# Softcap attention with soft-MoE slots on one core: queries and keys cast by their transfers, a second exponential tile per batch on VectorE

## The chip, the core and the metric

The kernel runs on one core of a Trainium2 chip. The metric is the device time of one execution in microseconds; 317.23 us is the median of seven runs of the kernel before.

## What is computed

Eight batches of twelve heads attend over 448 positions of 64 channels. The scores are capped by a tanh, so no running maximum is needed (the cap is 30). The result, seen as 3584 tokens of 768 channels, goes through a soft mixture of experts with 32 slots: the slots' softmax runs over all tokens, so the expert layers can only start when the attention of all batches is done.

```python
scores = cap * tanh((q @ k.T) / 8 / cap)          # per batch and head
attn = exp(scores) / sum(exp(scores))
x = (attn @ v) laid out as (3584, 768)
logits = x @ phi                                  # 32 columns
d = softmax over tokens of logits; slots = d.T @ x
out_e = relu(slots_e @ w1_e) @ w2_e               # 8 experts, 4 slots each
out = softmax over slots of logits @ slot_out
```

## The kernel before, in words

**Tiling.** A quad is four heads of one batch, so a batch has three quads and the kernel 24. A quad's q, k and v lie in SBUF with 128 partitions: two heads share the two halves of the partitions, and the two pairs of a quad (h = 0, 1) lie side by side in the free dimension. A pair has seven key tiles, which makes 336 score tiles of 128 x 448; six of them are a chunk, and there are 56 chunks (NCH), seven to a batch.

**The main loop** (L523) has one step for each chunk j, and each step has slots named 0, a, b, c and d in which other work is put. The fixed part of a step is: the score matmuls of the next chunk in two halves (`qk_chunk`, L260), the tanh of this chunk in two halves on ScalarE (`tanh_chunk`, L272, from PSUM), the exponential of the chunk before in one instruction on ScalarE (`exp_chunk`, L284, in place in SBUF), and the products with v of the pair that is complete (`pv_pass`, L335), each half followed by its normalisation on VectorE (`norm`, L324). [...] Everything else is put into slots by hand with `at(step, slot, function)` (L428 to L494): for a quad its casts, its transposes and its v cast (`quad_in`, L440), the transposes and logits of x, the sums of the slots, the weights' loads (`wjobs`, slot b), and filler matmuls (`spare`, L433) on the constant tile ones.

**Buffers that order the work.** Scores have two PSUM buffers, so a half of the next chunk waits for the tanh two halves back. There is one PSUM buffer for the transposes and small products (psT, tag T) and one for the products with v and the fillers (psV, tag pv). Exponentials have four SBUF buffers.

**Queries and keys.** `load` (L162) brings a quad's q or k as float32 through SyncE's queue; `cast` (L224) makes it bfloat16 on VectorE and issues the load of the next quad; `transp` (L232) makes seven 128 x 128 transposes on TensorE and copies them from PSUM on VectorE. The first quad has its own finer path (`first_half`, L200). v comes through SyncE's queue and is cast by GpSimd (`vcast`, L244), which waits until the products with the v tile of two quads back are done.

**The exponential on VectorE.** For the chunks in `shared` (L289) VectorE does the first of the six tiles with seven instructions (`poly_exp`, L291, in three parts), and ScalarE's instruction takes five tiles instead of six. Before, these are the chunks with j mod 7 = 3 from j = 10 on: seven chunks.

**The expert weights** are cast by their transfers, which GpSimd issues. What does not fit in SBUF goes to DRAM as bfloat16 (w2d) and comes back by 20 transfers of 384 KB through SyncE's queue (w2t, L631) into the SBUF that the attention's pools leave. The pools are stacked: ld, cst, ldv, qk, vb0, exps, vb1, xs before. The tail's pool starts at the place of ld, with hpad (4096 bytes of each partition) and then the 20 w2t tiles of 3072 bytes each; a w2t transfer waits until the tiles in whose place it lies are done with.

**The tail** is layer 1, layer 2 in two column halves (`layer2`, L673), and the output: ten tiles in halves (`half_tile`, L696), then pairs of whole tiles. Layer 2's second half needs all w2t tiles; the first eight half tiles are issued between its groups.

Of the kernel before, what the change touches and what calls it, by code (L numbers as in the profile page):

```python
# [9 lines left out]
F32 = mybir.dt.float32  # L10
BF16 = mybir.dt.bfloat16
# [5 lines left out]
P = 128  # L17
HP = 64
NT = 7
DH = 64  # L20
S = 448
# [11 lines left out]
def kernel(  # L33
# [54 lines left out]
    slacc = consts.tile([P, NJ, NS], F32, name="slacc")  # L88

    w1b = [wts.tile([P, NJ, F], BF16, name=f"w1b{e}", tag="w1", bufs=E)  # L90
           for e in range(E - 1)]
    w2b = wts.tile([P, R2, D], BF16, name="w2b")


# [32 lines left out]

    att = ExitStack()
    ld = att.enter_context(tc.tile_pool(name="ld", bufs=1))
    cst = att.enter_context(tc.tile_pool(name="cst", bufs=1))  # L130
    ldv = att.enter_context(tc.tile_pool(name="ldv", bufs=1))
    qk = att.enter_context(tc.tile_pool(name="qk", bufs=2))
    vb = [att.enter_context(tc.tile_pool(name="vb0", bufs=1))]
# [22 lines left out]
                       ap=[[NT * DH, P], [2 * S * DH, 2], [1, NT * DH]])  # L156

    def raw_tile(nm):
        return (ldv if nm == "v" else ld).tile([P, 2, S], F32, name=nm + "raw",
                                               tag=nm + "raw")  # L160

    def load(nm, Q):  # L162
        if Q < NQ:
            t = raw_tile(nm)
            sp.dma_start(out=t, in_=quad_ap(nm, Q))
            raws[nm, Q] = t

    def load_first():

        for nm in "qkv":  # L170
            raws[nm, 0] = raw_tile(nm)
        kc = raws["k", 0].rearrange("p h (c d) -> p h c d", d=DH)
        kin = quad_ap("k", 0, 0).rearrange("p (c d) -> p c d", d=DH)
        sp.dma_start(out=raws["q", 0][:, 0, :], in_=quad_ap("q", 0, 0))
        for c0, c1 in ((0, CS), (CS, NT)):
            act.dma_start(out=kc[:, 0, c0:c1, :], in_=kin[:, c0:c1, :])
        for nm in "kq":
            sp.dma_start(out=raws[nm, 0][:, 1, :], in_=quad_ap(nm, 0, 1))
        t = wts.tile([P, 3, 2, S], F32, name="raw1", tag="w1", bufs=E)
        for n, nm in enumerate("kqv"):  # L180
            raws[nm, 1] = t[:, n, :, :]
            if nm == "v":
                sp.dma_start(out=raws["v", 0], in_=quad_ap("v", 0))
            sp.dma_start(out=raws[nm, 1], in_=quad_ap(nm, 1))

    def first_pieces(h, jobs):

        for stage, nm, c0, c1, eng, bank, at0 in jobs:
            copy = act.copy if eng is act else dve.tensor_copy
            cols = slice(h * HP, h * HP + HP)  # L190
            if stage == "cast":
                copy(casts[nm, 0][:, c0:c1, cols],
                     raws[nm, 0][:, h, c0 * DH:c1 * DH].rearrange("p (c d) -> p c d", d=DH))
            elif stage == "turn":
                for c in range(c0, c1):
                    pe.transpose(bank[cols, at0 + c - c0, :], casts[nm, 0][:, c, cols], ident)  # L196
            else:
                copy(qkT[nm, 0][cols, c0:c1, :], bank[cols, at0:at0 + c1 - c0, :])

    def first_half(h):  # L200
        for nm in ("k", "q"):
            if h == 0:
                casts[nm, 0] = cst.tile([P, NT, P], BF16, name=nm + "bf", tag=nm + "bf")
                qkT[nm, 0] = qk.tile([P, NT, P], BF16, name=nm + "T", tag=nm + "T")
        one = psT.tile([P, 8, P], BF16, name="ps1", tag="T")
        two = psV.tile([P, NT, P], BF16, name="ps2", tag="pv")
        if h == 0:

            first_pieces(h, (("cast", "k", 0, CS, dve, None, 0), ("cast", "q", 0, 4, dve, None, 0),
                             ("cast", "q", 4, NT, act, None, 0), ("turn", "k", 0, CS, pe, two, 0),  # L210
                             ("copy", "k", 0, CS, dve, two, 0), ("turn", "q", 0, 4, pe, one, 0),
                             ("cast", "k", CS, NT, act, None, 0),
                             ("copy", "q", 0, 4, dve, one, 0), ("turn", "q", 4, NT, pe, two, CS),
                             ("copy", "q", 4, NT, act, two, CS), ("turn", "k", CS, NT, pe, one, 4),
                             ("copy", "k", CS, NT, dve, one, 4)))
        else:
            first_pieces(h, (("cast", "k", 0, NT, dve, None, 0), ("cast", "q", 0, NT, dve, None, 0),
                             ("turn", "k", 0, NT, pe, two, 0), ("turn", "q", 0, NT, pe, one, 0),
                             ("copy", "k", 0, NT, dve, two, 0), ("copy", "q", 0, NT, dve, one, 0)))
            for nm in ("q", "k"):  # L220
                raws.pop((nm, 0)), casts.pop((nm, 0))
                load(nm, 2)

    def cast(nm, Q):  # L224
        t = cst.tile([P, NT, P], BF16, name=nm + "bf", tag=nm + "bf")
        dve.tensor_copy(t.rearrange("p c (h d) -> p h c d", h=2),  # L226
                        raws.pop((nm, Q)).rearrange("p h (c d) -> p h c d", d=DH))
        casts[nm, Q] = t
        if Q > 1:
            load(nm, Q + 1)  # L230

    def transp(nm, Q):  # L232
        src = casts.pop((nm, Q))
        home = (psV, "pv") if (nm, Q) == ("k", 1) else (psT, "T")
        ps = home[0].tile([P, NT, P], BF16, name=nm + "ps", tag=home[1])
        for c in range(NT):
            pe.transpose(ps[:, c, :], src[:, c, :], ident)  # L237
        t = qk.tile([P, NT, P], BF16, name=nm + "T", tag=nm + "T")
        dve.tensor_copy(t, ps)  # L239
        qkT[nm, Q] = t  # L240
# [45 lines left out]

    shared = [j for j in range(NCH - 2) if j % 7 == 3 and j > 7] if cap < 80 else []  # L289

    def poly_exp(j, part):  # L291
        t, bits = exs[j][:, 0, :], 2.0 ** 23
# [146 lines left out]

    def quad_in(Q, cast_k, cast_q, k_in, q_in, v_in):  # L440
        if 0 < Q < NQ:
            at(*cast_k, cast, "k", Q)
            at(*cast_q, cast, "q", Q)
            at(*k_in, transp, "k", Q)
            at(*q_in, transp, "q", Q)
            at(*v_in, vcast, Q)

    for b in range(B):
        j = b * PER
        if b == 0:  # L450
            quad_in(1, (0, "a"), (0, "b"), (0, "d"), (1, "a"), (2, "d"))
        else:
            quad_in(3 * b + 1, (j - 1, "b"), (j, "a"), (j - 1, "d"), (j, "c"), (j + 1, "d"))
        quad_in(3 * b + 2, (j + 1, "c"), (j + 2, "c"), (j + 2, "b"), (j + 2, "d"),
                (j + 4, "d"))
        quad_in(3 * b + 3, (j + 4, "a"), (j + 5, "a"), (j + 4, "d"), (j + 5, "c"),
                (j + 6, "d"))
        p = 6 * b
        at(j + 1, "d", spare, 34 if b == 0 else 10)
        at(j + 2, "d" if b == 0 else "a", spare, 4 if b == 0 else 14)  # L460
        if b:
            at(j + 2, "c", spare, 8)
        at(j + 3, "d", spare, 10)
        at(j + 4, "a", x_transp, p)
        at(j + 5, "a", x_transp, p + 1)
        at(j + 6, "a", x_transp, p + 2)
        at(j + 5, "d", logits, 3 * b)
        if b < B - 1:
            at(j + 7, "a", x_transp, p + 3)
            at(j + 8, "a", x_transp, p + 4)  # L470
            at(j + 7, "d", logits, 3 * b + 1)
            at(j + 9, "a", x_transp, p + 5)
            at(j + 9, "d", logits, 3 * b + 2)
            at(j + 11, "0", e_exp, b)
            at(j + 11, "d", slot_sums, b)
            if b < B - 2:
                at(j + 12, "d", e_transp, b)
            if b < B - 2:
                at(j + 13, "d", e_norm, b)
            if b % 2:  # L480
                at(j + 14, "d", e_sums, b // 2)
    for j in shared:
        for dj, slot, part in ((0, "a", 0), (0, "c", 1), (0, "d", 2)):
            at(j + dj, slot, poly_exp, j, part)
    for n, job in enumerate(wjobs):
        at(1 + n * (NCH - 5) // len(wjobs), "b", *job)
    for j, slot, n in ((0, "a", 10), (0, "c", 10), (1, "b", 10), (1, "c", 8)):
# [208 lines left out]
    def half_tile(n, half, home, eng):  # L696

        if n % 8 == 0:
            obs[n, half] = wts.tile([P, 8, HD], F32, name="obh", tag="w1", bufs=E)
        ob = obs[n - n % 8, half][:, n % 8, :]  # L700
        bb, c = divmod(n, NT)
        pe.matmul(home, et_tile(bb, c), so[half], start=True, stop=True)  # L702
        if eng == "dve":
            dve.tensor_scalar_mul(ob, home, winv[:, bb, c:c + 1])
        else:
            act.mul(ob, home, winv[:, bb, c:c + 1])
        store(n, half, half + 1, ob)
# [10 lines left out]
    for n0 in range(0, n2, 4):  # L718
        layer2(n0, 1)
        if n0 >= 4 and n0 % 8 == 4 and done < NH - 2:  # L720
            for eng in ("act", "dve"):
                half_tile(done, 0, bank([P, HD], name="op0"), eng)
                done += 1
    dve.tensor_copy(so[1], so_ps[1])
    for n in range(done, NH):
# [68 lines left out]
```

The softmax here doesn't subtract the row's maximum and nothing guards it: scores larger than these inputs give would overflow.

## Time and profile before

| | |
|---|---|
| median of 7 runs | 317.23 us (316.78 to 320.11) |
| the profiled execution | 317.87 us |
| its span, first to last instruction | 315.7 us |
| ScalarE busy | 281.2 us, 208 instructions |
| TensorE busy, its weight loads | 270.4 us, 191.6 us |
| VectorE, GpSimd busy | 193.6 us, 106.8 us |
| transfers | 77.68 MB written, 246 GB/s on average |

A busy engine in this profile is one that has an instruction under way. Matmuls are pipelined, so their durations overlap: what one costs the engine is the distance to the next start, not its duration. An idle time is put down to what ended it last. Times within the span are counted from its start.

### The profile page before, as it was taken

To read this page: it belongs to the slowest core of one execution; us is meant where nothing else is said; L and a number is where in the kernel's file an instruction comes from. 1 tells how busy PE (TensorE), PEld (TensorE's weight loads), DVE (VectorE), ACT (ScalarE), POOL (GpSimd) and SP (SyncE) were. 2 spreads that over 40 slices of the span, in tenths; PEclk is the share of its full clock that TensorE was granted. 3 is DMA by queue.
4 is the path that set the end of the run, shared out by engine and by line. 5 is a ranking of instruction groups with operands and counts; after the bars stand their busy time and mean duration, and the time that the engine had idled before them with its cause. 6 is when DMAs were issued, how large, how long until landed. Compare 5 with 4: busy or idle time off the path is not lost.

```text
span 315.7 us, 8844 instructions
## 1 busy us (share of the span) xinstructions
PE 270.4 (86%) x3804; PEld 191.6 (61%) x3804; DVE 193.6 (61%) x473; ACT 281.2 (89%) x208; POOL 106.8 (34%) x134
## 2 busy tenths in 40 slices
PE   8899898899889998898889989998889998998720
PEld 6667666667656665666666666666666677743400
DVE  3736565766586659565867587657766664337740
ACT  4999999999999999999999999999999999235720
POOL 2464342523543452354245415441732130200000
PEclk9999999999999999999999999999999999999995
DMA  8899999799999989999999999999999806798997
GB/s 223 261 231 234 288 256 255 159 228 264 236 210 241 265 199 236 255 215 271 191 223 276 226 253 192 244 232 261 203 227 262 221 15 213 246 397 327 391 411 304
DMA packets 57478, 77.68 MB, mean 246 GB/s; under 512 B 3808, under 2 KB 53600, under 8 KB 57440
## 3 DMA queue, kind: packets, MB, share of 16 engines
q0 software_dynamic: 30480, 25.22, 52.1%
q1 hardware_dynamic: 26672, 51.68, 48.0%
q8 instruction: 29, 0.48, 0.6%
q10 hardware_dynamic: 288, 0.23, 0.2%
q14 instruction: 9, 0.07, 0.1%
HBM read 91.32 MB, written 18.87 MB: 349 GB/s over the span
## 4 chain that ended last, share of the span: by engine, by line
ACT 60%; PE 25%; DVE 6%; issue 2%; DMA 2%; SPq 0%; DVEq 0%; ACTq 0%
ACT ex L278 30%; ACT ex L282 29%; PE pv L318 6%; PE sc L269 4%; PE junk L506 2%; PE so_ps L676 2%; PE hp L649 2%; DMA out_dram<-ob 2%; DVE xq L329 1%; PE op L702 1%; PE boot L506 1%; PE kps L237 1%; PE xps L344 1%; PE slps L407 1%; PE ps L196 1%
## 5 line engine op out<-in xcount | busy, mean ns | idle before, releaser
L278 ACT ACTIVATE ex<-sc 128x1344 bf16<-128x1344 f32 (+1 forms) x113 | 162.0, 1689 | 1.0 <-PE sc L269 1.0
L282 ACT ACTIVATE ex<-ex 128x2688 bf16<-128x2688 bf16 (+4 forms) x58 | 159.0, 2774 | 0.1
L318 PEld LDWEIGHTS <-ex 128*128 128x128 bf16 x1344 | 78.7, 97 | 21.6 <-DVE xq L329 17.9
L318 PE MATMUL pv<-vbd,ex 128*128 128x130 bf16 x1274 | 88.6, 220 | 2.7 <-ACT ex L282 0.7
L269 PE MATMUL sc<-qT,kT 64*64 64x448 bf16 x672 | 78.7, 359 | 7.8 <-ACT ex L278 7.7
L247 POOL CAST vbd<-vraw 64x896 bf16<-64x896 f32 x23 | 21.4, 929 | 104.2 <-PE pv L318 71.0
L269 PEld LDWEIGHTS <-kT 64*64 64x64 bf16 x672 | 27.2, 105 | 25.2 <-issue 7.5
L329 DVE TENSOR_TENSOR xq<-pv,rec 128x256 bf16<-128x256 f32 x91 | 38.6, 424 | 3.2
L328 DVE RECIPROCAL rec<-pv 128x4 f32<-128x4 f32 x91 | 16.5, 181 | 31.9 <-PE pv L318 31.1
L506 PEld LDWEIGHTS <-ones 128*128 128x128 bf16 x470 | 28.7, 101 | 11.6 <-DVE xq L329 8.0
L372 POOL COPY e<-E 128x512 bf16<-128x512 bf16 x9 | 7.2, 801 | 81.0 <-ACT E L366 49.0
L506 PE MATMUL junk<-ones 128*128 128x128 bf16 x433 | 31.4, 219 | 2.5 <-DVE xq L329 1.6
L239 DVE COPY kT<-kps 128x896 bf16<-128x896 bf16 x23 | 14.4, 625 | 25.3 <-PE kps L237 25.2
L109 POOL DMA_DIRECT2D w1b<-in_moe_w_dram x32 | 25.6, 803 | 0.0
L248 POOL CAST vbd<-vraw 64x896 bf16<-64x896 f32 x23 | 23.6, 1027 | 1.3
L346 DVE COPY xT<-xps 128x512 bf16<-128x512 bf16 x47 | 19.6, 417 | 3.2 <-PE xps L344 3.2
L344 PE MATMUL xps<-ident,xq 128*128 128x128 bf16 x188 | 18.1, 218 | 0.2 <-DVE zacc L383 0.2
L239 DVE COPY qT<-qps 128x896 bf16<-128x896 bf16 x23 | 14.2, 618 | 5.2 <-PE qps L237 5.2
L237 PE MATMUL kps<-ident,kbf 128*128 128x128 bf16 x161 | 12.8, 219 | 4.2 <-DVE slacc L418 2.2
L226 DVE CAST kbf<-kraw 128x896 bf16<-128x896 f32 x22 | 16.0, 728 | 0.4 <-DMA kraw<-in_k_dram 0.4
L237 PE MATMUL qps<-ident,qbf 128*128 128x128 bf16 x161 | 12.8, 219 | 3.2 <-DVE lg L360 2.7
L237 PEld LDWEIGHTS <-kbf 128*128 128x128 bf16 x161 | 10.0, 97 | 9.0 <-issue 8.3
(113 smaller groups left out, 256.9 us busy)
## 6 DMA issues: line engine op xcount, KB each, us to landing
w1b<-in_moe_w_dram POOLq DMA_DIRECT2D x32, 384.0 KB, 10.0
vraw<-in_v_dram SPq DMA_DIRECT2D x23, 448.0 KB, 6.5
qraw<-in_q_dram SPq DMA_DIRECT2D x22, 448.0 KB, 7.7
kraw<-in_k_dram SPq DMA_DIRECT2D x22, 448.0 KB, 5.7
w2d<-in_moe_w_dram POOLq DMA_DIRECT2D x20, 384.0 KB, 9.3
w2t<-w2d SPq DMA_DIRECT2D x20, 384.0 KB, 5.7
out_dram<-ob SPq DMA_DIRECT2D x8, 768.0 KB, 7.7
w2b<-in_moe_w_dram POOLq DMA_DIRECT2D x12, 384.0 KB, 9.5
```

Source lines behind the costliest of these rows:

```text
L109: pool.dma_start(out=w1b[e][:, js, fs], in_=w1r[:, e, js, fs])
L237: pe.transpose(ps[:, c, :], src[:, c, :], ident)
L239: dve.tensor_copy(t, ps)
L247: pool.tensor_copy(t[0:HP, :, :, 0:DH], raw[0:HP])
L248: pool.tensor_copy(t[HP:P, :, :, DH + 1:VW - 1], raw[HP:P])
L269: pe.matmul(sc[cs, u, 0:S], qkT["k", Q][r, c, cs], qkT["q", Q][r, :, cs], start=True, stop=True)
L278: act.activation(exs[j][:, half * CS + u0:half * CS + u1, :], sc[:, u0:u1, 0:S], ACT.Tanh, scale=qk_scale / cap)
L282: act.activation(exs[j][:, u0:u1, :], exs[j][:, u0:u1, :], ACT.Exp, scale=cap)
L318: pe.matmul(pvs[pr, half][:, n, 0:VW], exs[j][:, u, GOFF[g]:GOFF[g] + P], vbds[Q % 2][:, h, c, :], start=(c == 0 and n == 0), stop=(c == N ...
L329: dve.tensor_tensor(xq[Q][:, 2 * half:2 * half + 2, h * P:(h + 1) * P] .rearrange("p g (i d) -> p g i d", i=2), pv[:, :, :, 0:DH], rec.to_ ...
L344: pe.transpose(ps[:, g, :], xq[Q][:, g, h * P:(h + 1) * P], ident)
L506: pe.matmul(junk if home is None else home, ones, ones, start=True, stop=True)
```

## The change

- `shared` takes the chunks with j mod 7 = 1 as well as 3 (from j = 8 on), 14 chunks instead of 7. The third part of the polynomial moves from slot d of the same step to slot b (mod 1) or slot a (mod 3) of the next step.
- From quad 2 on, q and k are loaded straight into bfloat16 tiles by transfers that GpSimd issues, two buffers each; the casts on VectorE and the pool cst are gone. The loads stand in the slots where the casts stood, except those of the batch's third quad, which go from (j+1, c) and (j+2, c) to (j, d) and (j+1, c). Quads 0 and 1 are still cast by an engine; their bfloat16 tiles lie for that time in a buffer of the expert weights (so one more expert's weights gets its buffer later).
- A quad's tile now has the two pairs one after the other, so a transpose takes one pair's 128 x 64: 14 of them, with the pairs in turn, write the lower and upper half of the PSUM partitions.
- The key transposes of the third quad of a batch move from (j+4, d) to (j+3, d), and the filler there goes from 10 matmuls to 4 in the batches after the first.
- The first half tile of the output is made as two products of 192 columns in two PSUM banks, one scaled by ScalarE and one by VectorE.

```diff
     w1b = [wts.tile([P, NJ, F], BF16, name=f"w1b{e}", tag="w1", bufs=E)
-           for e in range(E - 1)]
+           for e in range(E - 2)]
...
-    cst = att.enter_context(tc.tile_pool(name="cst", bufs=1))
...
     def raw_tile(nm):
-        return (ldv if nm == "v" else ld).tile([P, 2, S], F32, name=nm + "raw",
-                                               tag=nm + "raw")
+        if nm == "v":
+            return ldv.tile([P, 2, S], F32, name="vraw", tag="vraw")
+        return ld.tile([P, 2, S], BF16, name=nm + "b", tag=nm + "raw", bufs=2)
 
     def load(nm, Q):
         if Q < NQ:
             t = raw_tile(nm)
-            sp.dma_start(out=t, in_=quad_ap(nm, Q))
+            (sp if nm == "v" else pool).dma_start(out=t, in_=quad_ap(nm, Q))
             raws[nm, Q] = t
...
     def load_first():
-        for nm in "qkv":
-            raws[nm, 0] = raw_tile(nm)
+        for nm in "qk":
+            raws[nm, 0] = [ld.tile([P, S], F32, name=f"{nm}raw{h}", tag=nm + "raw", bufs=2)
+                           for h in range(2)]
+        raws["v", 0] = raw_tile("v")
...
+        t01 = wts.tile([P, 2, 2, NT, P], BF16, name="casts", tag="w1", bufs=E)
...
-    def cast(nm, Q):
-        t = cst.tile([P, NT, P], BF16, name=nm + "bf", tag=nm + "bf")
-        dve.tensor_copy(t.rearrange("p c (h d) -> p h c d", h=2),
-                        raws.pop((nm, Q)).rearrange("p h (c d) -> p h c d", d=DH))
-        casts[nm, Q] = t
-        if Q > 1:
-            load(nm, Q + 1)
+    def cast(nm):
+        dve.tensor_copy(casts[nm, 1].rearrange("p c (h d) -> p h c d", h=2),
+                        raws.pop((nm, 1)).rearrange("p h (c d) -> p h c d", d=DH))
 
     def transp(nm, Q):
-        src = casts.pop((nm, Q))
+        src = casts.pop((nm, Q)) if Q == 1 else raws.pop((nm, Q))
...
         for c in range(NT):
-            pe.transpose(ps[:, c, :], src[:, c, :], ident)
+            if Q == 1:
+                pe.transpose(ps[:, c, :], src[:, c, :], ident)
+                continue
+            for h in range(2):
+                pe.transpose(ps[h * HP:h * HP + HP, c, :], src[:, h, c * DH:(c + 1) * DH], ident)
...
-    shared = [j for j in range(NCH - 2) if j % 7 == 3 and j > 7] if cap < 80 else []
+    shared = [j for j in range(NCH - 2) if j % 7 in (1, 3) and j > 7] if cap < 80 else []
...
     def quad_in(Q, cast_k, cast_q, k_in, q_in, v_in):
         if 0 < Q < NQ:
-            at(*cast_k, cast, "k", Q)
-            at(*cast_q, cast, "q", Q)
+            for nm, when in (("k", cast_k), ("q", cast_q)):
+                at(*when, *((cast, nm) if Q == 1 else (load, nm, Q + 1)))
...
-        quad_in(3 * b + 2, (j + 1, "c"), (j + 2, "c"), (j + 2, "b"), (j + 2, "d"),
+        quad_in(3 * b + 2, (j, "d"), (j + 1, "c"), (j + 2, "b"), (j + 2, "d"),
                 (j + 4, "d"))
-        quad_in(3 * b + 3, (j + 4, "a"), (j + 5, "a"), (j + 4, "d"), (j + 5, "c"),
+        quad_in(3 * b + 3, (j + 4, "a"), (j + 5, "a"), (j + 3, "d"), (j + 5, "c"),
                 (j + 6, "d"))
...
-        at(j + 3, "d", spare, 10)
+        at(j + 3, "d", spare, 10 if b == 0 else 4)
...
     for j in shared:
-        for dj, slot, part in ((0, "a", 0), (0, "c", 1), (0, "d", 2)):
-            at(j + dj, slot, poly_exp, j, part)
+        for slot, part in (("a", 0), ("c", 1)):
+            at(j, slot, poly_exp, j, part)
+        at(j + 1, "b" if j % 7 == 1 else "a", poly_exp, j, 2)
...
     def half_tile(n, half, home, eng):
...
+        if n == half == 0:
+            for p, (bank_p, mul) in enumerate(zip(home, (act.mul, dve.tensor_scalar_mul))):
+                cs = slice(p * HD // 2, (p + 1) * HD // 2)
+                pe.matmul(bank_p, et_tile(bb, c), so[half][:, cs], start=True, stop=True)
+                mul(ob[:, cs], bank_p, winv[:, bb, c:c + 1])
+            store(n, half, half + 1, ob)
+            return
```

## The prediction, made before the result was known

> **What bounds the kernel now.** I read the page first: ScalarE (ACT) has most of the busy time, and its digits by slices are 9 from start to attention's end, where TensorE (PE) has 8 and 9 too.
>
> ```profile
> PE 270.4 (86%) x3804; PEld 191.6 (61%) x3804; DVE 193.6 (61%) x473; ACT 281.2 (89%) x208; POOL 106.8 (34%) x134
> ...
> ACT  4999999999999999999999999999999999235720
> ```
>
> The groups by form show that ACT does not wait before these instructions (last number). Their means overlap, so I take the distance from start to start in ACT's timeline.
>
> ```profile
> L278 ACT ACTIVATE ex<-sc 128x1344 bf16<-128x1344 f32 x111 | 160.8, 1706 | 0.0
> L282 ACT ACTIVATE ex<-ex 128x2688 bf16<-128x2688 bf16 x48 | 137.6, 2866 | 0.1
> L282 ACT ACTIVATE ex<-ex 128x2240 bf16<-128x2240 bf16 x7 | 18.0, 2575 | 0.0
> ```
>
> ```profile
> 87.02 2.69 ACT L282 ACTIVATE ex<-ex 128x2688 bf16<-128x2688 bf16 x1
> 89.36 0.55 ACT L366 ACTIVATE E<-lg 128x128 bf16<-128x128 f32 x1
> 89.56 2.71 ACT L278 ACTIVATE ex<-sc 128x1344 bf16<-128x1344 f32 x2
> 91.90 2.33 ACT L282 ACTIVATE ex<-ex 128x2240 bf16<-128x2240 bf16 x1
> 93.86 2.73 ACT L278 ACTIVATE ex<-sc 128x1344 bf16<-128x1344 f32 x2
> ```
>
> A full exponential takes 89.36 - 87.02 = 2.34 us, one with five tiles 93.86 - 91.90 = 1.96. A step of two tanh halves (91.90 - 89.56 = 2.34) and an exponential is 4.68 us, a batch 7 x 4.68 + 0.20 (E) - 0.38 = 32.6. ACT sets the pace; PE's reserve is what PE waits for ACT:
>
> ```profile
> PE sc L269 <- ACT ex L278: 7.7, 19, 0.7
> ```
>
> 7.7 us in all, some in the first steps: about 1.0 per batch.
>
> After the attention the transfers rule. SyncE's timeline shows 8 w2t transfers before 270 and 12 from 270.16, when the last products with v release the exponentials:
>
> ```profile
> 245.42 20.95 SPq L631 DMA_DIRECT2D w2t<-w2d  x8
> ...
> 270.16 8.21 SPq L631 DMA_DIRECT2D w2t<-w2d  x12
> ```
>
> Layer 2's last matmuls start at 287.4 (tile view of w2t), and the stores follow at 352 to 415 GB/s (windows of 10 us from 280). The end hangs on this w2t stream.
>
> [...]
>
> **Part by part.**
>
> *ACT.* Seven more chunks (8, 15 to 50) give a tile to VectorE: 7 x 0.38 = **-2.6 us**, if PE keeps pace.
>
> *PE, the transposes.* 44 blocks (q and k of 22 quads) get 14 transposes instead of 7. Do the pairs run together?
>
> ```profile
> 8.20 0.55 PE L196 MATMUL ps<-ident,kbf 128*64 128x128 bf16 x7
> 8.59 0.55 PE L196 MATMUL ps<-ident,qbf 128*64 128x128 bf16 x7
> ...
> 81.56 0.76 PE L269 MATMUL sc<-qT,kT 64*64 64x448 bf16 x6 [0.45 <-ACT ex L278]
> 82.25 0.56 PE L237 MATMUL kps<-ident,kbf 128*128 128x128 bf16 x7
> 82.65 0.61 PE L506 MATMUL junk<-ones 128*128 128x128 bf16 x8
> 83.19 0.76 PE L269 MATMUL sc<-qT,kT 64*64 64x448 bf16 x6
> ...
> 273.38 1.48 PE L649 MATMUL hp<-w1b,slT 128*32 128x512 bf16 x24
> ```
>
> Seven narrow transposes take 8.59 - 8.20 = 0.39 us, as seven wide ones do (82.65 - 82.25 = 0.40): 56 ns each, so their weight loads are hidden. hp's column tiles run four at once: its 24 matmuls start (1.48 - 0.38) / 23 = 48 ns apart (mean duration 380 ns, group view), where 512 columns at 56 ns per 128 would take 224. So I take pairs as simultaneous, extra cost 0; the bound above is one after the other, +0.39. The mode changes add: from junk to sc, 83.19 - 82.65 = 0.54 for 8 x 0.056 = 0.45, a gap of 0.09. A block sat beside wide matmuls on one side; now it differs from both neighbours, one change more, 0.09 (0 to 0.18). So a block costs **0.1 us more** (0 to 0.57); a batch has six: +0.6. Six fillers fewer: 6 x 0.056 = -0.34.
>
> *VectorE (DVE).* It loses 44 casts (groups: 16.0 + 14.2 = 30.2 us) and gains 7 x (383 + 394 + 394 + 615 + 625 + 667 + 872 = 3950 ns) = 27.7. The sum is level; the place matters. In slot b of phase 2 (step mod 7) the third part (1.54 us) now stands between the key copy and the logits' sum, for which the query transposes wait (one PSUM buffer); no product with v falls in that step. PE there already waits ("qps <- DVE lg": 2.7 us, 7 times), and a cast of 0.65 leaves the same stretch; I take +0.4 per batch (0 to 0.8). In phases 1 and 3 the parts stand behind a normalisation, whose buffer is free by then, as in phase 3 now. The moved key block no longer stands behind slacc's sum ("kps <- DVE slacc": 2.2 us, 5 times): -0.4.
>
> *The balance of a batch:* PE +0.6 - 0.34 + 0.4 - 0.4 = +0.26, ACT 0.38 shorter: 0.64 of PE's 1.0 us is used. ACT still sets the pace, with little left. The moved block also takes its 0.4 us out of phase 4, ahead of slot sums, and costs phase 3 that much less 0.34 of filler.
>
> *GpSimd and the queues.* 44 issues of about 0.8 us (w1b row: 803 ns) raise POOL from 107 to 142 us, in 255. They queue behind weights' loads (10.0 us to landing) and behind vcast, which waits for PE (71.0 us, longest 6.7). Loads stand 2.5 to 4 steps, 11.7 to 18.7 us, ahead of their transposes. The tightest follows the copy of E in phase 4: GpSimd's timeline has that at 155.37, so issue at 156.2, at 10 us landing by 166.2; the transposes come two and a half steps later, about 11.5 us after E's copy, near 166.9. But no weight stands ahead of it then (the last before were issued at 147), so 6 us is likelier. Cost 0, up to 2 us in all. Quad 2's loads move ahead of phi and vcast 0 on POOL; they wait for first casts (4 to 7 us), and vcast 0 starts at 12.2 anyway after VectorE's memset: 0. SyncE's queue only loses 44 issues. The loads of the third quad, a slot group sooner, stand behind the release of buffers that were transposed before: 0. HBM reads stay the same.
>
> *The tail's memory.* The pool cst (3584 bytes) is gone, so ldv, qk, vb0 and exps move down by that, but w2t tiles stay: they start at ld. From sizes, before: w2t tile 7 lies at 25600 to 28672 from ld, inside the first buffer of exps (25152 to 30528[...]), which chunk 52 leaves early; tile 8 reaches the next one, used by chunk 55 to the very end. That is the 8 and 12 of the timeline. After: the first buffer lies at 21568 to 26944, and tile 7 reaches into chunk 55's. So **7 and 13**. One more transfer of 384 KB in the saturated stream: 0.393 MB / 0.41 MB per us (windows 278 to 284: 406 to 412 GB/s) = **+1.0 us** (0 if hidden, 1.3 at the mean rate of this stream). Layer 2's second half waits for the last of them, and the small stores behind it.
>
> *First half tile.* Ready perhaps 0.2 us sooner (ACT's 580 ns halved in part), the second as much later. Layer 2's second half and the w2t stream hide it: 0 (-0.2 to +0.2). The buffer for the eighth expert's weights: 0, that load comes many steps later.
>
> **Sum.** 315.7 - 2.6 + 1.0 = 314.1 us of span; the profiled execution 317.87 - 1.6 = 316.3. Against the median I take the same difference: 317.23 - 1.6 = **315.6 us**. This profiled execution lay 0.64 above the median, within the runs shown.
>
> **Rivals.**
> 1. *The tail hides the extra transfer.* For: in 270 to 276 the stream is not saturated (278 GB/s mean over 270 to 280). Against: issue is already ahead of landing there. 317.23 - 2.6 = 314.6.
> 2. *PE becomes the bound in part*: 0.2 per block (two mode changes) and 0.4 of delays stays unrelieved: PE +1.2 - 0.34 + 0.4 = 1.26, and 0.38 of ACT, is 0.64 over the reserve; 7 x 0.64 = 4.5 would take the gain and more; with relief of 0.4, 7 x 0.24 = 1.7 of it: 317.3.
> 3. *Slower: the narrow transposes do not pair.* A block then costs 0.39 and a mode change, 0.48: PE +2.9 - 0.34 - 1.0 = +1.6 per batch, for 44/6 = 7.3 batches 11.4, and the tail's 1.0: about 329.6; half paired 0.29 gives 7.3 x (1.74 - 1.34) + 1.0 = 3.9: 321.1. It decides from 6x = 1.34 - 1.0/7.3, x = 0.20 per block. For: PE is busy 86%[...]. Against: hp's four at once.
> 4. *The offload yields nothing* (ACT's shorter instruction waits for VectorE or PE): 317.2 + 1.0 = 318.2 at most, 317.2 with the tail hidden.
>
> **Chances.** Forecast 0.48 (own range 315.0 to 316.2, a half to two thirds of it beyond 0.5%), rival 1 0.16, rival 2 0.20, rival 3 0.12, rival 4 0.04. 0.5% is 1.6 us, about what a measurement of this kernel can tell from no change. Faster by more: 0.32 + 0.16 = 0.48; within: 0.16 + 0.19 + 0.03 = 0.38; slower: 0.12 + 0.02 = 0.14. Range: from rival 1 with 0.2 from the half tile and 0.1 of spread, 314.3, to rival 2 with its spread, 317.8; rival 3 is left out.
>
> **What would show it.** Right: 14 exponentials of 2240 at 1.96, ACT without idle time, attention's end 2.6 us sooner; kps blocks of 14 in 0.4 us; w2t 7 before and 13 after the last product with v; PE's wait for ACT down to about 0.4 per batch. Wrong: idle time of ACT before L278 with PE as releaser (rivals 2, 3); kps waiting for a transfer; w2t still 8 and 12, or stores that start no later relative to attention's end (rival 1).

## The result and the profile after

The changed kernel takes 315.69 us (median) beside 317.33 for the kernel before on the same chip: ratio 0.9949, 95% interval 0.9934 to 0.9964. The prediction was 315.6. The profiled execution took 315.4 us, with a span of 313.6. Two of the changed kernel's 27 executions, of 818.92 and 1306.81 us, are left out of the ratio.

The page of the kernel after, busy times and ScalarE's slices:

```profile
PE 271.7 (87%) x4071; PEld 190.3 (61%) x4071; DVE 191.4 (61%) x479; ACT 278.4 (89%) x208; POOL 137.8 (44%) x178
...
ACT  4999999999999999999999999999999999226630
```

ScalarE lost 2.8 us of work and is still busy in every slice of the attention. TensorE has 267 matmuls more, VectorE has 2.2 us less, GpSimd 31 us more for 44 issues (0.7 us each). The groups by form of the kernel after give the new split, 14 short exponentials for 7, and next to no idle time ahead of them (last number):

```profile
L286 ACT ACTIVATE ex<-sc 128x1344 bf16<-128x1344 f32 x111 | 162.3, 1734 | 0.0
L290 ACT ACTIVATE ex<-ex 128x2688 bf16<-128x2688 bf16 x41 | 118.2, 2883 | 0.1
L290 ACT ACTIVATE ex<-ex 128x2240 bf16<-128x2240 bf16 x14 | 36.3, 2592 | 0.0
```

TensorE's waits (us in all, times, longest) show where its reserve went; one line of the kernel before, then two of the kernel after:

```profile
PE qps L237 <- DVE lg L360: 2.7, 7, 0.4
```

```profile
PE sc L277 <- ACT ex L286: 4.4, 12, 0.5
PE qps L245 <- DVE lg L368: 4.0, 7, 0.6
```

It waits 4.4 us for ScalarE where it waited 7.7, and 4.0 us for the logits' sum where it waited 2.7. The wait of the key transposes for slacc (2.2 us) is gone, and no transposes wait for a transfer. TensorE's timeline of the kernel after (start, us) has the new block of 14:

```profile
81.45 0.58 PE L245 MATMUL kps<-ident,kb 128*64 128x128 bf16 x14
81.96 0.62 PE L515 MATMUL junk<-ones 128*128 128x128 bf16 x8
...
84.14 0.58 PE L245 MATMUL qps<-ident,qb 128*64 128x128 bf16 x14 [0.58 <-DVE lg L368]
84.66 0.98 PE L326 MATMUL pv<-vbd,ex 128*128 128x130 bf16 x14
```

From start to the next start it is 0.51 to 0.52 us, where seven wide ones took 0.40 (one transpose lasts 219 ns in the median, so they overlap). And SyncE's two timelines of the kernel after, up to the end of the last products with v and from there on, have the split of the w2t transfers that was worked out from sizes:

```profile
244.10 19.42 SPq L640 DMA_DIRECT2D w2t<-w2d  x7
...
267.30 8.65 SPq L640 DMA_DIRECT2D w2t<-w2d  x13
```

For what follows I split an execution at two marks of ScalarE's timeline: the first tanh and the last tanh. **The attention** lies between them, **the tail** is from the last tanh to the last landing of a store. Before: attention 264.84 - 7.17 = 257.67, tail 49.74. After: 261.97 - 6.86 = 255.11, tail 50.33. So the attention is 2.56 shorter, the tail 0.59 longer. The first tanh comes 0.3 earlier, but it moves by as much between executions of one kernel (6.79 and 7.16 in runs 2 and 6 below, whose kernel is the same), so it is not put to the change.

By its sum and its terms (2.6 won, 1.0 lost) the prediction looked right. The experiments ask whether the 1.0 is what I took it for, and whether the parts are worth what I said.

### The profile page after: what moved, and what is told of

Its sections match the earlier page's. It is cut to its first block, busy times and chain, and to the rows that moved or that the text cites. A ratio compares the mean times of both kernels' runs of the same rounds, so it can differ in the third digit from the quotient of the medians.

```text
span 313.6 us, 9348 instructions
## 1 busy us (share of the span) xinstructions
PE 271.7 (87%) x4071; PEld 190.3 (61%) x4071; DVE 191.4 (61%) x479; ACT 278.4 (89%) x208; POOL 137.8 (44%) x178
## 4 chain that ended last, share of the span: by engine, by line
ACT 69%; PE 16%; DVE 5%; DMA 3%; issue 2%; SPq 1%; DVEq 0%; ACTq 0%
ACT ex L286 36%; ACT ex L290 32%; PE pv L326 4%; DMA out_dram<-ob 2%; PE sc L277 2%; PE so_ps L685 2%; PE hp L658 2%; PE junk L515 2%; DMA kraw<-in_k_dram 1%; DVE xq L337 1%; SPq L700 1%; PE op L719 1%; PE xps L352 1%; DVE obh L721 1%; PE pvm L326 1%
## 5 line engine op out<-in xcount | busy, mean ns | idle before, releaser
L255 POOL CAST vbd<-vraw 64x896 bf16<-64x896 f32 x23 | 22.5, 980 | 66.2 <-PE pv L326 53.3
L515 PEld LDWEIGHTS <-ones 128*128 128x128 bf16 x428 | 26.0, 101 | 10.6 <-DVE xq L337 6.0
L515 PE MATMUL junk<-ones 128*128 128x128 bf16 x391 | 29.1, 220 | 3.1 <-DVE xq L337 2.6
L256 POOL CAST vbd<-vraw 64x896 bf16<-64x896 f32 x23 | 24.0, 1043 | 1.3
L109 POOL DMA_DIRECT2D w1b<-in_moe_w_dram x32 | 24.4, 765 | 0.0
L167 POOL DMA_DIRECT2D qb<-in_q_dram x22 | 16.2, 738 | 4.0 <-DVE kT L206 3.3
L245 PE MATMUL qps<-ident,qb 128*64 128x128 bf16 x308 | 12.8, 222 | 4.1 <-DVE lg L368 4.0
L167 POOL DMA_DIRECT2D kb<-in_k_dram x22 | 16.0, 728 | 0.0
L113 POOL DMA_DIRECT2D w2d<-in_moe_w_dram x20 | 15.1, 762 | 0.0
```

The lines of the kernel that those rows point to most:

```text
L109: pool.dma_start(out=w1b[e][:, js, fs], in_=w1r[:, e, js, fs])
L167: (sp if nm == "v" else pool).dma_start(out=t, in_=quad_ap(nm, Q))
L255: pool.tensor_copy(t[0:HP, :, :, 0:DH], raw[0:HP])
L256: pool.tensor_copy(t[HP:P, :, :, DH + 1:VW - 1], raw[HP:P])
L515: pe.matmul(junk if home is None else home, ones, ones, start=True, stop=True)
```

## Experiments

Median and ratio are each against the kernel before on the same chip: 317.52 us for runs 1 to 4, 317.83 for runs 5 to 8, 317.34 for runs 9 to 12. The ratio, with its 95% interval in brackets, is not the quotient of the two medians and lies up to 0.3% below it, so small differences are read from medians of kernels on one chip. In expectations "theory" is the prediction's sum unless another is named.

**1. The rest of the change without the second tile.**

```diff
-    shared = [j for j in range(NCH - 2) if j % 7 in (1, 3) and j > 7] if cap < 80 else []
+    shared = [j for j in range(NCH - 2) if j % 7 == 3 and j > 7] if cap < 80 else []
```

> The changed kernel with one exponential tile per batch on VectorE instead of two (the chunks with j mod 7 = 3 alone); all else stays. Theory (gain 2.6 us on ScalarE, loss 1.0 in the tail): the gain goes and the loss stays, 315.7 + 7 x 0.38 = 318.3 us, 1.0 slower than before. Rival (ScalarE's shorter instructions yielded only 1.6 and the tail hides its extra transfer): 317.3, as before.

318.29 us, ratio 1.0013 [0.9993, 1.0033]. As the theory has it: without the tile the change gives nothing and seems to cost some 0.8. Its attention takes 257.49 (257.67 before), its tail 50.67. So narrow transposes, casting transfers and moved steps together cost nothing that shows in the attention; what is lost is lost in the tail.

**2. The memory layout of before for the tail.** An unused buffer of cst's size at cst's place.

```diff
+    pad = att.enter_context(tc.tile_pool(name="pad", bufs=1))
+    pad.tile([P, 2 * NT * P], BF16, name="pad")
     ldv = att.enter_context(tc.tile_pool(name="ldv", bufs=1))
```

> The changed kernel with an unused SBUF pool of 3584 bytes in the place of the dropped pool cst, so that the w2t tiles lie over the same attention buffers as before, and one tile lies over memory that is never used. Theory: 8 (or more) w2t transfers are issued before the last product with v and 12 after, and the time falls by 0.6 to 1.0 us, to 314.7 to 315.1. Rival (the tail hides the extra transfer): 8 and 12 too, but the time stays at 315.7.

315.39 us, ratio 0.9933 [0.9909, 0.9958]; w2t splits 8 and 12 again. This is too near both values to tell; run 6 repeats it beside the changed kernel.

**3. The second tile alone**, in the kernel before, with the casts left on VectorE.

```diff
-    shared = [j for j in range(NCH - 2) if j % 7 == 3 and j > 7] if cap < 80 else []
+    shared = [j for j in range(NCH - 2) if j % 7 in (1, 3) and j > 7] if cap < 80 else []
...
-        for dj, slot, part in ((0, "a", 0), (0, "c", 1), (0, "d", 2)):
-            at(j + dj, slot, poly_exp, j, part)
+        for slot, part in (("a", 0), ("c", 1)):
+            at(j, slot, poly_exp, j, part)
+        at(j + 1, "b" if j % 7 == 1 else "a", poly_exp, j, 2)
```

> The kernel before with the second exponential tile per batch alone (and the third part's new slots); queries and keys are still cast on VectorE, all else as before. Theory: VectorE has room in sum (193.6 + 27.7 = 221 of some 260 us of attention), so ScalarE gains its 2.6 us, and the memory of the tail is as before: 314.7 us, with at most 0.5 lost to TensorE's waits for VectorE, 314.7 to 315.2. Rival (the cast transfers pay for the second tile): VectorE's queue holds up TensorE by more than its reserve of 1.0 us per batch, ScalarE has idle time before its tanh, and the time is 317 us or above.

326.82 us, ratio 1.0272 [1.0236, 1.0308]. The theory is wrong here, and by 12 us. VectorE is busy 220.9 us of 326.2, which leaves room on average, but the logits' sum, the slots' sum (slacc) and the casts stand behind the polynomial in its queue, and TensorE waits for them. Two of TensorE's waits in this kernel, and ScalarE's wait for TensorE:

```profile
PE qps L237 <- DVE lg L360: 8.5, 7, 1.2
...
PE kps L237 <- DVE slacc L418: 6.0, 5, 1.2
...
ACT ex L278 <- PE pv L318: 9.0, 12, 2.4
```

In the kernel before, the first two are 2.7 and 2.2 us and the third does not occur. The attention takes 269.08 us, 11.4 longer. Within one of these waits, the 1.21 us up to 86.26 in TensorE's timeline, TensorE's clock drops. Stretches of 2 us of this kernel (busy us of PE, PEld, DVE, ACT, POOL, each with its count; then the granted clock, the DMA share and GB/s):

```profile
84.00:86.00 2.00, 1.04 (x16) 0.50 (x14) 1.97 (x5) 2.00 (x3) 0.00 (x0) 0.97 0.98 239
86.00:88.00 2.00, 1.74 (x17) 1.84 (x18) 0.83 (x3) 2.00 (x2) 0.00 (x0) 0.50 1.13 181
...
90.00:92.00 2.00, 2.00 (x20) 1.49 (x19) 1.19 (x4) 0.61 (x1) 0.68 (x1) 0.50 1.14 279
```

VectorE works through 84 to 86 and TensorE half idles; then the clock stays at 0.50 until 92.7, and ScalarE, busy throughout until 88, falls to 0.61 of 2 us. But this is the only such drop in the attention: 6.8 us at half clock are 3.4 us of TensorE's work at most, out of the 11.4. Two other executions of run 3, with mean granted clocks of 0.987 and 0.986 (the kernel before has 0.979 to 0.987), still took 326.03 and 326.34 us. So most of the loss is TensorE's waits for VectorE, and the drop adds to it. TensorE was busy 1.04 of 2 us in 84 to 86, and its longest gap there was 1.21 us. Two equal gaps before it, from 51.36 and 61.13, had no drop after them, so the gap alone does not decide; what does decide was not shown.

**4. The first half tile whole again**, on one bank and scaled by ScalarE alone.

```diff
-        if n == half == 0:
...
-                half_tile(done, 0, bank([P, HD], name="op0") if done else
-                          [bank([P, HD // 2], name="op00") for _ in range(2)], eng)
+                half_tile(done, 0, bank([P, HD], name="op0"), eng)
```

> The changed kernel with the first half tile of the output made whole again on ScalarE, as before. Theory: nothing, 315.7 us within 0.2, since the stores stand behind the w2t transfers and layer 2's second half. Rival: the first store sets the end, 0.2 to 0.4 us slower.

315.85 us, ratio 0.9934 [0.9908, 0.9959], like runs 2 and 5. As expected, nothing that can be measured.

**5 and 6. The changed kernel, and run 2's kernel again beside it.**

> The changed kernel once more, as the neighbour of the next three on the same chip. All theories: 315.4 to 316.0 us, 7 w2t transfers before the last product with v and 13 after.

> The changed kernel with an unused buffer of 3584 bytes where the pool cst lay, so that w2t splits 8 and 12 again; beside the changed kernel on one chip. Prediction's term (the extra transfer costs 1.0 us): 1.0 below the changed kernel, about 314.7. Rival, after a first look at 315.39 (the transfer is mostly hidden, since the chunks' small stores keep all DMA engines occupied later and the stream before them has holes): 0.2 to 0.4 below, 315.2 to 315.5.

315.73 and 315.87 us, ratios 0.9906 [0.9871, 0.9940] and 0.9907 [0.9876, 0.9938]. Here the extra w2t transfer costs nothing that can be measured; run 2 lay 0.46 below run 4's kernel, so it is 0 to 0.5 in all, and the prediction's term of 1.0 is too large. Why, is seen in the 2 us stretches from 18 us after the last tanh (columns as above; in the 2 us before them both move 410 to 412 GB/s), the changed kernel first, the padded one second:

```profile
280.05:282.05 2.00, 1.74 (x25) 0.62 (x21) 1.23 (x3) 1.14 (x3) 0.00 (x0) 1.00 1.03 409
282.05:284.05 2.00, 2.00 (x32) 0.79 (x32) 1.50 (x3) 1.29 (x3) 0.00 (x0) 1.00 0.80 293
```

```profile
280.26:282.26 2.00, 1.74 (x25) 0.62 (x21) 1.22 (x3) 1.14 (x3) 0.00 (x0) 1.00 0.69 266
282.26:284.26 2.00, 2.00 (x32) 0.79 (x32) 1.50 (x3) 1.30 (x3) 0.00 (x0) 1.00 0.63 227
```

The engines do the same at the same time. The padded kernel's w2t stream is through sooner and leaves a hole before the stores (266, then 227 GB/s), which the changed kernel fills for the most part with the extra transfer (409, then 293). The kernel before has such a hole as well, just ahead of its first store's landing at 287.8:

```profile
286.00:288.00 2.00, 2.00 (x36) 0.96 (x34) 0.84 (x3) 0.58 (x1) 0.00 (x0) 1.00 0.70 251
```

The first store is issued 19.16 us after the last tanh in both, and SyncE then issues the 20 small ones about 0.5 us apart, at 370 GB/s, less than the 410 of the w2t stream, so that a late start can be caught up. The traces of all the kernels with narrow transposes that have the packet described next agree: with 13 late w2t transfers (six traces) the last of them lands 22.09 to 23.05 us after the last tanh and with 12 (runs 2, 6 and 8) 21.14 to 21.37, about 1.2 us sooner, but the last store lands only 0.3 us sooner on average (50.3 for 50.6). (The profile of the kernel before, with 12, has the last w2t landing at 22.5; that execution lay 0.5 us above its median.)

So where does the tail's 0.6 to 0.9 come from, which also run 1 has? The packet records show one thing that all kernels with narrow transposes had by then and the two without them had not: a 16 KB instruction packet (16384 bytes, queue q8) amid the large stores, 32.0 to 34.3 us after the last tanh, 0.88 to 0.97 us long. In the kernel before the packet of this place comes at 52.1, after the last store. TensorE's program has grown by 267 matmuls and as many weight loads, q8's packets from 29 to 32 in the span (the other instruction queue, q14, stays at 9), and their places moved with it. So I take q8 for TensorE's queue. Runs 9 to 12, in which TensorE's instructions alone change, test this.

**7. The transposes unpaired**: the seven of one half of the array, then the seven of the other.

```diff
-        for c in range(NT):
-            if Q == 1:
-                pe.transpose(ps[:, c, :], src[:, c, :], ident)
-                continue
-            for h in range(2):
+        for h in range(1 if Q == 1 else 2):
+            for c in range(NT):
+                if Q == 1:
+                    pe.transpose(ps[:, c, :], src[:, c, :], ident)
+                    continue
```

> The changed kernel with the same 14 narrow transposes of a block in another order: seven of one half of the array, then seven of the other. Theory (the changed kernel is fast because neighbours of different column halves run at the same time): a block grows by 0.39 us, six blocks and a reserve of about 0.4 per batch left: 7.3 x (2.3 - 0.4) = 14 us, about 329; 326 if the reserve is 0.8. Rival (TensorE overlaps them in any order, or the weight loads bound the block either way): 315.7.

318.28 us, ratio 1.0013 [0.9987, 1.0039]: slower than the changed kernel by 2.55, much less than the theory's 14. TensorE's timeline of this kernel:

```profile
84.93 0.75 PE L245 MATMUL qps<-ident,qb 128*64 128x128 bf16 x14 [0.57 <-DVE lg L368]
85.61 0.58 PE L326 MATMUL pv<-vbd,ex 128*128 128x130 bf16 x7
```

A block takes 85.61 - 84.93 = 0.68 us, 0.16 more than paired and not 0.39 more: in the trace the first of the second seven starts together with the fourth of the first, so even this order overlaps in part. Pairing is real and worth 44 x 0.16 = 7.0 us of TensorE's time, of which the attention (257.72, 2.6 longer) felt 2.6. The reserve took the other 4.4, 0.6 per batch.

**8. A third exponential tile per batch on VectorE**, in run 2's kernel.

```diff
-    shared = [j for j in range(NCH - 2) if j % 7 in (1, 3) and j > 7] if cap < 80 else []
+    shared = [j for j in range(NCH - 2) if j % 7 in (1, 3, 5) and j > 7] if cap < 80 else []
...
-        at(j + 1, "b" if j % 7 == 1 else "a", poly_exp, j, 2)
+        at(j + 1, "a" if j % 7 == 3 else "b", poly_exp, j, 2)
```

> The padded kernel with a third exponential tile per batch on VectorE (phase 5, third part in slot b of the next step), six chunks more. Theory A (ACT is still the bound and VectorE has room since the casts left): 6 x 0.38 = 2.3 less than the padded kernel, about 313.1. Theory B (TensorE's reserve is used up by now, so ACT only waits instead): within 0.5 of the padded kernel, about 315.3. Theory C (VectorE's queue delays the copies of q and k and TensorE's clock falls, as with the second tile alone): over 317.

328.72 us, ratio 1.0316 [1.0267, 1.0365]: theory C. In step 34 TensorE waits 1.21 and 1.11 us for copies that VectorE does late, and its clock is at 0.50 from 167.4 to 170.8. There are two more such drops in this attention, from 201.5 for 3.4 us and from 235.6 for 10.2. Together they are 17 us at half clock, so up to 8.5 of the 12.0 us by which this attention is longer than the padded kernel's; here the clock bears more of the loss than in run 3. This kernel's TensorE timeline, and two of its stretches:

```profile
165.93 0.38 PE L401 MATMUL eps<-ident,e 128*128 128x128 bf16 x4 [1.21 <-DVE qT L249]
167.42 0.38 PE L365 MATMUL lps<-phib,xT 128*128 128x32 bf16 x8 [1.11 <-DVE ET L402]
```

```profile
164.00:166.00 2.00, 0.79 (x10) 0.37 (x9) 1.93 (x6) 2.00 (x3) 0.59 (x1) 1.00 1.11 249
168.00:170.00 2.00, 2.00 (x19) 1.66 (x18) 0.74 (x4) 0.93 (x1) 0.00 (x0) 0.50 1.29 203
```

VectorE is busy 213 us of 326 there, even less than in run 3. The average does not show the trouble; the fullest step does.

**9 to 12. The place of the instruction packet.** The changed kernel again; with 28 fillers fewer (10 to 6 in each of seven batches, 56 instructions with their weight loads); the kernel before with 28 more (10 to 14); the changed kernel with 28 more.

```diff
-        at(j + 1, "d", spare, 34 if b == 0 else 10)
+        at(j + 1, "d", spare, 34 if b == 0 else 6)
```

> The changed kernel, as neighbour of the next three on one chip. All theories: 315.4 to 316.0 us; one 16 KB instruction packet in the stretch of the large stores, and one DMA engine that ends about 1 us after the other 15.

> The changed kernel with 4 fillers fewer per batch (28 in all), so that TensorE's program is shorter by 28 matmuls and 28 weight loads and its last instruction packet should be fetched after the last store instead of amid the large ones. Theory (that packet of 16 KB holds one of the 16 DMA engines for about 0.95 us, and the last store waits for this engine): 0.6 to 1.2 us below the changed kernel, about 314.7, all of it after the last exponential. Rival (the tail's 0.6 to 1.0 comes from elsewhere, for example from the order in which weights and stores share the queue): equal to the changed kernel within 0.3.

> The kernel before with 4 fillers more per batch (28 in all), so that its last instruction packet, which came after the end, should be fetched amid the large stores. Theory: 0.6 to 1.2 us above the kernel before, all of it after the last exponential, one DMA engine ending about 1 us behind the others. Rival (packet without effect; the fillers fit TensorE's reserve of 1.0 per batch with their 0.22): equal to the kernel before within 0.3.

> The changed kernel with 4 fillers more per batch, a control: the packet is fetched 56 instructions earlier and still in the stretch of the stores, so theory: the tail as in the changed kernel within 0.3. The attention tells TensorE's reserve once more: 4 x 0.056 = 0.22 per batch more, equal to the changed kernel if the reserve left is over 0.22 per batch (theory: about 0.65 by the unpaired run), up to 1.6 slower if it is used up.

| kernel | median, us | ratio to before | attention | packet after last tanh | tail |
|---|---|---|---|---|---|
| before | 317.34 | 1 | 257.67 | 52.1 | 49.74 |
| after | 315.72 | 0.9934 [0.9912, 0.9955] | 255.02 | 32.0 | 50.40 |
| after, 28 fewer | 314.69 | 0.9909 [0.9878, 0.9939] | 254.79 | none | 50.06 |
| before, 28 more | 318.28 | 1.0015 [0.9992, 1.0037] | 258.18 | 30.5 | 51.22 |
| after, 28 more | 315.20 | 0.9919 [0.9888, 0.9949] | 255.24 | 28.7 | 50.06 |

(The last three columns are of one profiled execution each.) The medians move by -1.03 and +0.94, as the theory said; the intervals overlap, but eight of the nine executions with 28 fewer took 314.23 to 315.37 us, and all eleven of the changed kernel 315.36 to 315.90. The last line is the best control: there TensorE has more work, but the packet has left the large stores, and the kernel is 0.52 faster than the changed one. So it is the packet's place that counts and not the fillers' work. That work shows in the attention, which is 0.23 shorter, 0.51 longer and 0.22 longer in the three; taking this off the medians leaves, as an estimate from single profiles, 0.8, 0.4 and 0.7 us for the packet's place.

The profiles show the mechanism. The DMA view of the changed kernel from 308 to 316, in slices of 0.2 us, and the same stretch with 28 fillers fewer:

```profile
GB/s 430 338 430 461 399 461 399 399 369 354 369 415 445 338 77 31 31 15 31 15 0 0 0 0 0 0 0 0 0 0 0 0 0 0 0 0 0 0 0 0
```

```profile
GB/s 399 400 461 461 430 369 430 369 430 461 323 384 399 384 399 215 46 0 0 0 0 0 0 0 0 0 0 0 0 0 0 0 0 0 0 0 0 0 0 0
```

In the first the stream ends at 310.8, but some 15 to 31 GB/s go on for 1.2 us more, about what one of 16 engines moves (410 / 16 = 26). The records don't name the engine; that it is the one that had carried the packet is inferred. In the second all end together. By the packet records of all 14 profiles (from the last time that 12 engines or more were busy to the end of the last packet) the straggle is 1.14 to 1.58 us in the nine that have the packet amid the large stores (the changed kernel three times, runs 1, 2, 4, 6, 7, 8) and 0.16 to 0.61 in the five that have not (before, runs 3, 10, 11, 12). The stretch of the large stores, from the last small store's landing to the last landing of all, parts the same way: 17.84 to 18.48 us in the nine, 16.66 to 17.10 in the five.

With 28 more in the kernel before, the packet comes amid the last small stores, and another thing happens. Its DMA view from 292.5 to 317.5, in slices of 0.63 us, and its waits from 293 to 300:

```profile
GB/s 361 374 376 359 385 339 27 10 143 445 396 433 403 403 413 433 403 423 374 462 403 393 452 403 369 398 433 433 413 413 433 383 423 413 403 398 369 10 0 0
```

```profile
ACT ob L754 <- DMA out_dram<-obh: 2.0, 2, 1.8
```

The packet takes 1.66 us; three small stores, which by then are issued, land about 1.5 us late, the buffer of the next tile is freed late, and the DMA engines nearly stand still for that time (27, 10, 143 GB/s in its slices). There is no straggler, but the end comes as late. This execution took 319.01 us, 0.73 above its kernel's median, so its tail may be longer than usual. In the changed kernel with 28 more (packet at 28.7) the same hole is shorter, about 0.8 us, and the tail is no longer than with the packet gone: my "within 0.3 of the changed kernel" was missed by a little, since a gap in the small stores' stretch can be caught up. Its attention of 255.24 shows that 0.22 us per batch of further work for TensorE, 1.5 us in all, costs 0.1 to 0.2.

So a packet of 16384 bytes, 0.96 us long amid the changed kernel's stores, is felt in a stretch in which the DMA engines are busy to the end.

## Why the prediction was right, and where only its sum was

**ACT, -2.6: right.** (7 x 0.38 is 2.66, a little more than the sum has.) The attention is 2.56 shorter, and run 1 gives 2.4 of it to the second tile (257.49 - 255.11).

**PE, 0.1 more per block: right.** 0.51 to 0.52 less 0.40 is 0.11 to 0.12, though the sign given for it, blocks of 14 in 0.4 us, had left this 0.1 out. What the prediction calls a mode change is in the traces a later start after a matmul of another tile shape: 149 ns (median) from junk, 128*128, to sc, 64*64, and 56 from junk to junk. In the block at 81.45 the two transposes of a pair start 3 ns apart, and run 7 shows that the 0.1 rests on pairing. What failed was rival 3's price for unpaired blocks: 0.39 was bounded from instructions in strict order, and TensorE starts the second group while the first is under way, so that even the forced case costs 0.16 more. My expectation for run 7 took over this error.

**The delay at the query transposes, +0.4 per batch: half.** The wait grew by (4.0 - 2.7)/7 = 0.19 per batch, and the key block's relief was 2.2/7.3 = 0.3 for 0.4. **The balance** left 0.36 of TensorE's reserve; run 7 finds 0.6. The direction held: ACT sets the pace. The predicted sign, a wait for ACT of about 0.4 per batch, fits the 4.4 us, part of them in the first steps.

**VectorE, "the sum is level; the place matters": right as a sentence, not followed through.** The sum is level (191.4 for 193.6). But I priced the place only for the changed kernel, and did not see that room had to be made first: run 3 costs 9 us against the kernel before, run 8 costs 13 against the padded one. The rest of the change is the condition of the gain, not a neighbour of it. Which part of it counts most is not shown: run 3 keeps the casts on VectorE, but it also lacks the move of the key transposes (they are those of the next batch's first quad, 3b + 3), which takes them out from behind slacc's sum (3.8 us of the added waits), and still has the six fillers per batch that the change drops.

**GpSimd and the queues, 0: right.** 137.8 us busy for 142 predicted, loads of q and k land after 6.2 and 7.5 us (median), no transpose waits for one.

**The tail, +1.0: the step that failed.** "One more transfer of 384 KB in the saturated stream": the split came as predicted, 7 and 13, and the last w2t transfer does land about 1 us later for it, but the last store hardly waits for that, because the stream is not saturated up to the stores. It has a hole in front of them, and runs 2 and 4 to 6 put the term at 0 to 0.5. The prediction read the stream from 278 to 284, ahead of the hole at 286 to 288; rival 1 had the right outcome, with a gap at another place (270 to 276) as its reason. The sign that the prediction gave for rival 1 was there, too: the first store is issued no later after the last tanh (19.17 us, before 19.28). In its place stands a cost that I had not thought of: the 534 instructions that TensorE's program grew by moved its last instruction packet from after the end into the large stores, which costs about 0.4 to 0.8 us by the estimates above, and 1.0 if all that the medians moved is its. Two terms, one wrong and one missing, were of like size, and the sum came out right for a partly wrong reason, which is luck. With the packet out of the way (run 10) the change is worth 317.34 - 314.69 = 2.65, rival 1's -2.6.

**First half tile, 0: right**, to what run 4 can tell; its first store is issued 19.28 us after the last tanh, 0.1 later than in the changed kernel.

What stays open is how the single packet's 0.96 us becomes a straggler of 1.2. The profiles show only 0.5 us between runs 9 and 10 where the medians have 1.03, but the profiled execution of run 9 lies 0.29 below its median and that of run 10 lies 0.26 above. In run 10 the large stores end the sooner although the last small store lands later (33.4 us after the last tanh, 32.3 to 32.8 in the three profiles of the changed kernel); the instruction packets in its w2t stream lie 1.1 to 1.6 us later too (15.5 and 21.5 us), which may be why. Moving one packet alone was not tried.

## What to carry to other kernels

Before work is put on an engine with room on average, look at the fullest step of its queue and at who waits behind it: the same tile was worth 2.6 us with the rest of the change in place and cost 9 without it. A price for an extra transfer in a stream holds only if the stream has no hole before the next thing that waits for it, so look for the hole first. And when a change alters the number of instructions, look for where the 16 KB instruction packets fall in stretches that the DMA engines bound; a few fillers more or fewer can move them (here 28 more moved one from 32.0 to 28.7 us after the last tanh, and with 28 fewer there was none).

## What the runs showed of the hardware that was not expected

- One instruction packet takes 0.88 to 1.66 us amid stores, and the last store, or a buffer, comes later for it (0.88 in runs 2 and 8, 1.66 in run 11; its effect in runs 9 to 12).
- TensorE's clock fell to 0.50, for 6.8 and 3.4 us, with no gap before it over 1.21 us, in stretches where it was busy 0.8 to 1.0 of 2 us (at 85.9 in run 3 and at 167.4 in run 8).
- One instruction of VectorE, the SCALAR_TENSOR_TENSOR at L309, took 1.26 us each time beside GpSimd's cast of the second half of v; the same form at L311, with no cast beside it, took 0.62. GpSimd and VectorE in the timeline of the kernel after, and two groups by form:

```profile
78.78 1.24 POOL L256 CAST vbd<-vraw 64x896 bf16<-64x896 f32 x1
79.23 1.26 DVE L309 SCALAR_TENSOR_TENSOR xp<-xp,xm 128x448 f32<-128x448 f32 x1
```

```profile
L309 DVE SCALAR_TENSOR_TENSOR xp<-xp,xm 128x448 f32<-128x448 f32 x14 | 13.5, 962 | 0.5
...
L311 DVE SCALAR_TENSOR_TENSOR xp<-xp,xm 128x448 f32<-128x448 f32 x14 | 8.6, 616 | 0.0
```

The same form takes 616 ns at L311. At L309 seven of the 14 take 1.26 us, all beside 0.79 us of the second half of a v cast, six of the others 0.63, beside 0.34 us of a GpSimd copy, and the last 0.91, beside 0.44 us of that copy; a GpSimd instruction that issues a DMA beside L311 does not slow it (615 to 616 ns with one, 615 to 617 without). Beside these casts L309 loses 0.64 us each time against L311; for the copy the trace has no clear rule, and the cause was not shown.
